# Key-value products of batches 5 to 7 in one quartered stretch with the attention products of batches 4 to 6, in a linear-attention and MLP kernel

## The chip, the cores and the metric

The kernel runs on one core of a Trainium2 chip. The metric is the device time of one launch in microseconds (us); of several executions the median is taken. In the text TensorE does the matmuls, VectorE (DVE in the profile) and ScalarE (ACT) the work on elements, GpSimd (POOL) some more of that, and SyncE (SP) issues most of the DMAs. Each engine takes its instructions in the order in which the program lists them; an instruction that waits holds up all that stand behind it on that engine.

## What is computed

```python
q_s = softmax of q over head_dim          # q, k, v: batch 8, heads 8, seq 576, head_dim 64, float32
k_s = softmax of k over seq
kv  = einsum('bhsd,bhse->bhde', k_s, v)
x   = einsum('bhsd,bhde->bhse', q_s, kv)  # then to (4608 tokens, 512)
h   = x @ w_in                            # 512 x 2048
g   = maximum(0.01 * h, h)
out = g @ w_out                           # 2048 x 512, float32
```

## The kernel before

**The two layers.** The 4608 tokens are taken in nine tiles of 512, t = 0 to 8. In a tile, layer 1 (`layer1`, L488) computes 16 blocks of 128 hidden units, j = 0 to 15: for each j four matmuls of 128x128 weights by 512 columns into one PSUM bank, `ph`, of a pool of six (`psB`). After each j, `leaky` (L497) on ScalarE makes the bf16 activation `gj` from it. Layer 2 (`layer2`, L509) then takes four row groups of 128 tokens, `tsub` = 0 to 3: for each, 16 matmuls, j = 0 to 15, each with `gj` as the weights, into one PSUM bank `pout` of a pool of two. `store` (L503) copies `pout` to `out_sb`, on VectorE nearly always, and SyncE writes it out with two DMAs. Row group 2 reuses the bank of row group 0, and 3 that of 1.

**The attention.** A tile t needs the attention output `xT` of the batches that its tokens lie in. A batch b has 576 tokens, so batch b is attended to in tile b - 1. Its path is this:

- `load_all`: three DMAs on SyncE's queue bring k, q and v of a batch (1152 KB each) into a pool of six raw buffers.
- `k_begin` and `q_begin` take buffers; `k_tree` (L150, four maxima on VectorE), `k_allmax` (L155 to L175, VectorE), `k_sub` (L183, subtract the maximum over the sequence; GpSimd here), `k_exp` (L191, one exponential of 2304 columns on ScalarE).
- `v_cast` (L203, twice 1152 columns, GpSimd): v in bf16, into one of two buffers `vb`.
- `q_max` (L214, VectorE), `q_sub` (L273; GpSimd here), `q_exp` (L281, ScalarE), `q_sum` (L290 and L292), `q_norm` (L297, both VectorE), `q_turn` (L481: a transposing DMA on SyncE's queue gives `qX`).
- `kv` (L310): the key-value product. 72 matmuls, each of 64x64 weights in one quarter of TensorE's array, by 65 columns (the 65th is a column of ones: it gives the softmax sums), into two PSUM banks `pkv`. `kd_make` (L329, L330; VectorE) divides by the sums: four small instructions.
- `attend_all` (L429): the attention product, 8 matmuls of 64x64 weights by 512 columns and 8 by 64, also in quarters, into six PSUM banks `po`. Six `x_keep` casts (L452, ScalarE) bring them to `xT`.

A "quartered stretch" in what follows is a run of such 64x64 matmuls between the 128x128 ones of the two layers.

**What sets the order.** It is written out by hand: `at(t, u, ...)` hangs functions on a place in tile t. u = 0 to 15 is the place right after the activation of j = u in layer 1; u = 16 + 4*tsub + i, i = 0 to 3, is in row group tsub of layer 2, after its matmul 4*i + 3. So u = 19, 23, 27 and 31 are the ends of the row groups, right after that group's `store`; u of 32 and more goes on into the next tile. The functions' instructions enter each engine's queue at that place. `plan(b, o)` hangs batch b's path from place o of tile b - 2 on: o is 27 for batch 3, 22 for batch 4, and 17 for 5 to 7. Batches 0 to 2 are set apart.

Of the kernel before, what the change touches and what calls it, by code (L numbers as in the profile page):

```python
# [8 lines left out]
FP32 = mybir.dt.float32  # L9
# [10 lines left out]
L = 64  # L20
R = 9
# [4 lines left out]
def kernel(  # L26
# [9 lines left out]
    nc = tc.nc  # L36
# [3 lines left out]
    B, H, S, D = q.shape  # L40
# [6 lines left out]
    P = 128  # L47
# [83 lines left out]
    def k_begin(b):  # L131
        st[b]["ke"] = ke_pool.tile([P, R, HL, D], BF16, name="ke")
        st[b]["kmax"] = mx_pool.tile([P, HL, D], FP32, name="kmax")
        st[b]["kmaxT"] = mx_pool.tile([P, HL * D], FP32, name="kmaxT")
        st[b]["kall"] = mx_pool.tile([P, HL, D], FP32, name="kall")

    def k_tree(b, hs, steps=slice(0, 4)):
        n = hs.stop - hs.start
        ks = st[b]["k"][:, hs]
        if steps.start == 0:  # L140
            st[b]["t4"] = mx_pool.tile([P, HL, 4, D], FP32, name="t4")[:, 0:n]
        t4 = st[b]["t4"]
        t2, t1 = t4[:, :, 0:2], t4[:, :, 0]
        for o, i0, i1 in (
            (t4, ks[:, :, 0:4], ks[:, :, 4:8]),
            (t2, t2, t4[:, :, 2:4]),
            (t1, t1, t4[:, :, 1]),
            (st[b]["kmax"][:, hs], t1, ks[:, :, 8]),
        )[steps]:
            nc.vector.tensor_tensor(out=o, in0=i0, in1=i1, op=ALU.max)  # L150

    def k_allmax(b):


        nc.vector.transpose(  # L155
            out=st[b]["kmaxT"], in_=st[b]["kmax"].rearrange("p h d -> p (h d)")
        )
        m2 = small_pool.tile([P, CB, 2], FP32, name="m2")
        nc.vector.tensor_reduce(
            out=m2[:, :, 0],  # L160
            in_=st[b]["kmaxT"].rearrange("p (c j) -> p c j", j=32),
            axis=AX.X,
            op=ALU.max,
        )
        for a in range(4):
            o = a ^ 1
            nc.vector.tensor_reduce(
                out=m2[32 * o : 32 * o + 32, :, 1],
                in_=m2[32 * a : 32 * a + 32, :, 0:1],
                axis=AX.X,  # L170
                op=ALU.max,
            )
        m = small_pool.tile([P, CB], FP32, name="m")
        nc.vector.tensor_reduce(out=m, in_=m2, axis=AX.X, op=ALU.max)
        nc.vector.transpose(  # L175
            out=st[b]["kall"].rearrange("p h d -> p (h d)"),
            in_=m.unsqueeze(2).to_broadcast([P, CB, 32]),
        )

    def k_sub(eng, b, hs):  # L180
        ks = st[b]["k"][:, hs]
        n = hs.stop - hs.start
        eng.tensor_tensor(  # L183
            out=ks,
            in0=ks,
            in1=st[b]["kall"][:, hs].unsqueeze(2).to_broadcast([P, n, R, D]),
            op=ALU.subtract,
        )

    def k_exp(b, hs):  # L190
        nc.scalar.activation(  # L191
            out=st[b]["ke"][:, :, hs].rearrange("p r h d -> p h r d"),
            in_=st[b]["k"][:, hs],
            func=AF.Exp,
        )

    def v_cast(eng, b, gg):
        o = vb2[b % 2][:, :, gg, :, 0:D].rearrange("p r h d -> p h r d")
        i = st[b]["v"][:, 2 * gg : 2 * gg + 2]
        if eng is nc.scalar:  # L200
            eng.copy(out=o, in_=i)
        else:
            eng.tensor_copy(out=o, in_=i)  # L203


    def q_begin(b):
        st[b]["qe"] = qe_pool.tile([P, R, HL, D], BF16, name="qe")
        if b < 2:
            st[b]["qT"] = qT_pool.tile([P, NB, R, L], BF16, name="qT", tag="qT")

    def q_max(b, rs, hs=ALLH):
        n, m = rs.stop - rs.start, hs.stop - hs.start
        st[b]["qmax", rs.start, hs.start] = o = small_pool.tile([P, HL, n], FP32, name="qmax")[:, 0:m]
        nc.vector.tensor_reduce(out=o, in_=st[b]["q"][:, hs, rs], axis=AX.X, op=ALU.max)  # L214
# [55 lines left out]
    def q_sub(eng, b, rs, hs=ALLH):  # L270
        n, m = rs.stop - rs.start, hs.stop - hs.start
        qs = st[b]["q"][:, hs, rs]
        eng.tensor_tensor(  # L273
            out=qs,
            in0=qs,
            in1=st[b]["qmax", rs.start, hs.start].unsqueeze(3).to_broadcast([P, m, n, D]),
            op=ALU.subtract,
        )

    def q_exp(b, rs, hs=ALLH):  # L280
        nc.scalar.activation(  # L281
            out=st[b]["qe"][:, rs, hs].rearrange("p r h d -> p h r d"),
            in_=st[b]["q"][:, hs, rs],
            func=AF.Exp,
        )

    def q_sum(b, rs, hs=ALLH):
        n, m = rs.stop - rs.start, hs.stop - hs.start
        qsum = small_pool.tile([P, n, HL], FP32, name="qsum")[:, :, 0:m]
        nc.vector.reduce_sum(out=qsum, in_=st[b]["qe"][:, rs, hs], axis=AX.X)  # L290
        st[b]["qrec", rs.start, hs.start] = qrec = small_pool.tile([P, n, HL], FP32, name="qrec")[:, :, 0:m]
        nc.vector.reciprocal(out=qrec, in_=qsum)  # L292

    def q_norm(b, rs, hs=ALLH):
        n, m = rs.stop - rs.start, hs.stop - hs.start
        qes = st[b]["qe"][:, rs, hs]
        nc.vector.tensor_tensor(  # L297
            out=qes,
            in0=qes,
            in1=st[b]["qrec", rs.start, hs.start].unsqueeze(3).to_broadcast([P, n, m, D]),  # L300
            op=ALU.mult,
        )
# [15 lines left out]
    def kv(b):  # L318

        pkv = [psB_pool.tile([P, 2, D + 2], FP32, name="pkv", tag=BANK_TAG) for _ in range(2)]  # L320
        for gg in range(2):
            kv_quads(b, gg, [pkv[hh][:, gg] for hh in range(2)])
        st[b]["pkv"] = pkv

    def kd_make(b):
        for hh in range(2):
            pkv = st[b]["pkv"][hh]
            krec = small_pool.tile([P, 2, 1], FP32, name="krec")
            nc.vector.reciprocal(out=krec, in_=pkv[:, :, D : D + 1])  # L329
            nc.vector.tensor_tensor(  # L330
                out=kd2[b % 2][:, :, hh],
                in0=pkv[:, :, 0:D],
                in1=krec.to_broadcast([P, 2, D]),
                op=ALU.mult,
            )
# [110 lines left out]
    def x_keep(eng, b, ggs, rows, hp):  # L446
# [6 lines left out]
        else:  # L453
            eng.tensor_copy(out=o, in_=ps)

    def attend_rows(b, rows, engs=(nc.scalar, nc.scalar)):
        groups = ((0, 1),) if rows.stop - rows.start <= 4 else ((0,), (1,))
        for ggs in groups:
            attend(b, ggs, rows)
        return [  # L460
            lambda ggs=ggs, hp=hp: x_keep(engs[hp], b, ggs, rows, hp) for ggs in groups for hp in range(2)
        ]
# [15 lines left out]
    def q_turn(b, rs=ALLR):  # L478
        if rs.start == 0:
            st[b]["qX"] = qT_pool.tile([P, R * 2, P], BF16, name="qX", tag="qT")  # L480
        nc.sync.dma_start_transpose(  # L481
            out=st[b]["qX"][:, 2 * rs.start : 2 * rs.stop],
            in_=st[b]["qe"][:, rs].rearrange("p r h d -> p (r h d)"),
        )
# [35 lines left out]
    def at(t, u, *fns):  # L520
        while t > 0 and u >= 32:
            t, u = t + 1, u - 32
        hooks.setdefault((t, u), []).extend(fns)
# [7 lines left out]
    def load_all(b):  # L531
        whole = [(ALLH, ALLR)]
        st[b]["k"] = load(k, b, "k_raw", whole)
        st[b]["q"] = load(q, b, "q_raw", whole)
        st[b]["v"] = load(v, b, "v_raw", whole)
# [98 lines left out]

    XR = (slice(0, 6), slice(6, R))
    for b in range(3, B):
        at(b - 2, 2, lambda b=b: load_all(b))

    def plan(b, o):
        t = b - 2  # L640
        at(t, o, lambda: k_begin(b), lambda: q_begin(b), lambda: k_tree(b, ALLH))
        at(t, o + 3, lambda: k_allmax(b), lambda: k_sub(nc.gpsimd, b, ALLH))
        at(t, o + 7, lambda: q_max(b, ALLR), lambda: q_sub(nc.gpsimd, b, ALLR))
        at(t, o + 11, lambda: k_exp(b, ALLH))
        at(t, o + 12, lambda: v_cast(nc.gpsimd, b, 0), lambda: v_cast(nc.gpsimd, b, 1))
        at(t, o + 16, lambda: q_exp(b, ALLR))
        at(t, o + 18, lambda: q_sum(b, ALLR))
        at(t, o + 21, lambda: q_norm(b, ALLR))
        kvu = o + (24 if b == 3 else 25)
        at(t, kvu, lambda: kv(b))  # L650
        at(t, kvu + 1, lambda: kd_make(b))
        at(t, o + 22, lambda: q_turn(b))
        at(b - 1, 27 if b < 5 else 23, lambda: attend_all(b, (slice(0, 8),), (slice(8, R),)))


    def plan2():
        b = 2
# [13 lines left out]
        at(2, 19, lambda: attend_all(b, (XR[1],)))  # L671

    plan2()
    for b in range(3, B):
        plan(b, {3: 27, 4: 22}.get(b, 17))


    def g_tiles():
# [125 lines left out]
```

## Time and profile before

| what | value |
|---|---|
| median of 3 runs | 284.82 us (284.78 to 285.58) |
| the profiled execution, its time | 285.1 us |
| its span, first to last instruction | 283.3 us |
| what lies around the span | 1.8 us |
| TensorE busy | 273.4 us, 96% |
| ScalarE, VectorE, GpSimd busy | 145.5, 142.5, 89.5 us |
| granted TensorE clock over the span | 0.998 |
| chain that ended last: lines L488 and L509 | 38% each |

A line of the timeline gives start, duration, engine, line of the code, operation, result and inputs, shape, and how many were merged; in brackets, how long the engine was idle before, and what released it. Merged pieces overlap a little in time, because instructions are pipelined. The long shares of TensorE's two layers on the chain say that most of the time is one matmul after another; what lies before tile 1 (loads and the first batches) is not touched by the change.

### The profile page before, as it was taken

Reading aid. Unit: us, or ns where it says so; the run is one execution under the profiler, and the core shown is the slowest. Engines: PE = TensorE matmul, PEld = TensorE weight load, DVE = VectorE, ACT = ScalarE, POOL = GpSimd, SP = SyncE. Lnnn points to the kernel's source line nnn. Section 1 sums busy time; section 2 is a strip of 40 time slices with the busy share of each in tenths; the row PEclk is TensorE's granted clock in tenths of the full one; section 3 lists DMA queues with packets and bytes.
Section 4 is the critical chain, followed back from the end, with each engine's and each line's share of the span. In section 5 each row is a group of like instructions: output and inputs, shape, how many; then the busy total and the mean of one; then the engine's idle time right before and its main releaser. Section 6 shows DMA issues by size and latency. Waiting matters only on the chain.

```text
span 283.3 us, 4965 instructions
## 1 busy us (share of the span) xinstructions
PE 273.4 (96%) x1995; PEld 133.3 (47%) x2022; DVE 142.5 (50%) x237; ACT 145.5 (51%) x258; POOL 89.5 (32%) x62
## 2 busy tenths in 40 slices
PE   8889999999999999999999999999999999999994
PEld 3378644444444544444444444444444444444443
DVE  3975984997860992597193718381711100110011
ACT  4976653775359336912973367435843165026400
POOL 2946660035078029308700680059000000000000
PEclk9999999999999999999999999999999999999999
DMA  7999999894969165943598349933052210230033
GB/s 242 335 208 337 285 179 390 264 345 168 174 161 398 31 144 154 405 90 76 119 402 140 74 84 387 188 76 73 1 86 65 61 24 0 65 81 6 0 76 74
DMA packets 37159, 45.81 MB, mean 162 GB/s; under 512 B 16016, under 2 KB 20368, under 8 KB 37136
## 3 DMA queue, kind: packets, MB, share of 16 engines
q1 hardware_dynamic: 33664, 41.16, 49.6%
q0 software_dynamic: 3312, 4.20, 8.4%
q8 instruction: 16, 0.26, 0.4%
q10 hardware_dynamic: 160, 0.13, 0.2%
q14 instruction: 7, 0.06, 0.1%
HBM read 36.70 MB, written 9.44 MB: 163 GB/s over the span
## 4 chain that ended last, share of the span: by engine, by line
PE 80%; DMA 11%; POOL 3%; ACT 2%; DVE 1%; issue 1%; SPq 0%; ACTq 0%; POOLq 0%
PE ph L488 38%; PE pout L509 38%; DMA w_out_sb<-in_moe_w_out_dram 4%; DMA w_in_sb<-in_moe_w_in_dram 3%; DMA k_raw<-in_k_dram 2%; PE po L429 2%; DMA qX<-qe 2%; PE pkv L310 2%; POOL w_in_sb L123 1%; ACT gj L497 1%; DVE qe L297 1%; DVE qsum L290 1%; POOL w_out_sb L128 1%; ACT qe L281 0%; POOL vb L203 0%
## 5 line engine op out<-in xcount | busy, mean ns | idle before, releaser
L488 PE MATMUL ph<-xT,w_in_sb 128*128 128x512 bf16 (+1 forms) x627 | 126.5, 357 | 1.3 <-DMA w_in_sb<-in_moe_w_in_dram 0.6
L509 PE MATMUL pout<-w_out_sb,gj 128*128 128x512 bf16 (+2 forms) x579 | 126.6, 373 | 1.1 <-DMA w_out_sb<-in_moe_w_out_dram 0.6
L497 ACT ACTIVATE gj<-ph 128x512 bf16<-128x512 f32 x144 | 81.3, 604 | 52.4 <-PE ph L488 52.0
L488 PEld LDWEIGHTS <-w_in_sb 128*128 128x128 bf16 x640 | 62.1, 98 | 62.2 <-DMA w_in_sb<-in_moe_w_in_dram 0.8
L509 PEld LDWEIGHTS <-gj 128*128 128x128 bf16 x592 | 56.3, 98 | 65.5 <-issue 1.0
L503 DVE COPY out_sb<-pout 128x512 f32<-128x512 f32 (+1 forms) x34 | 22.7, 675 | 88.6 <-PE pout L509 82.0
L183 POOL TENSOR_TENSOR k_raw<-k_raw,kall 128x2304 f32<-128x2304 f32 (+1 forms) x6 | 29.1, 4854 | 74.9 <-DVE kall L175 60.9
L452 ACT CAST xT<-po 128x512 bf16<-128x512 f32 (+3 forms) x43 | 17.0, 489 | 44.5 <-PE po L429 44.5
L273 POOL TENSOR_TENSOR q_raw<-q_raw,qmax 128x2304 f32<-128x2304 f32 (+4 forms) x12 | 32.3, 2692 | 22.9 <-DVE qmax L214 22.2
L290 DVE TENSOR_REDUCE qsum<-qe 128x36 f32<-128x2304 bf16 (+5 forms) x13 | 20.1, 1544 | 31.4 <-ACT qe L281 31.4
L297 DVE TENSOR_TENSOR qe<-qe,qrec 128x2304 bf16<-128x2304 bf16 (+5 forms) x13 | 22.1, 1698 | 0.4
L191 ACT ACTIVATE ke<-k_raw 128x2304 bf16<-128x2304 f32 (+2 forms) x11 | 17.6, 1602 | 7.8 <-POOL k_raw L183 5.2
L214 DVE TENSOR_REDUCE qmax<-q_raw 128x36 f32<-128x2304 f32 (+5 forms) x13 | 19.9, 1536 | 0.0
L281 ACT ACTIVATE qe<-q_raw 128x2304 bf16<-128x2304 f32 (+5 forms) x13 | 17.3, 1329 | 3.2 <-POOL q_raw L273 3.2
L203 POOL CAST vb<-v_raw 128x1152 bf16<-128x1152 f32 x14 | 15.9, 1166 | 0.0
L150 DVE TENSOR_TENSOR t<-k_raw 128x1024 f32<-128x1024 f32 (+1 forms) x10 | 10.1, 1006 | 2.0 <-DMA k_raw<-in_k_dram 1.8
L150 DVE TENSOR_TENSOR t<-t 128x256 f32<-128x256 f32 (+2 forms) x20 | 9.6, 478 | 0.6
L341 PE MATMUL pout<-zero 128*128 128x512 bf16 x23 | 8.1, 492 | 1.4 <-POOL zero L98 1.3
L503 ACT COPY out_sb<-pout 128x512 f32<-128x512 f32 (+1 forms) x3 | 1.6, 544 | 14.4 <-PE pout L509 14.4
L310 PEld LDWEIGHTS <-ke 64*64 64x64 bf16 x576 | 5.7, 106 | 3.2 <-ACT gj L497 1.7
L310 PE MATMUL pkv<-vb,ke 64*64 64x65 bf16 x576 | 6.8, 194 | 0.2
L228 ACT ACTIVATE qe<-q_raw,nmax 128x64 bf16<-128x64 f32 x16 | 5.3, 334 | 3.3 <-DVE nmax L223 3.3
(59 smaller groups left out, 90.4 us busy)
## 6 DMA issues: line engine op xcount, KB each, us to landing
out_dram<-out_sb SPq DMA_DIRECT2D x70, 128.0 KB, 2.4
v_raw<-in_v_dram SPq DMA_DIRECT2D x7, 1152.0 KB, 10.5
k_raw<-in_k_dram SPq DMA_DIRECT2D x6, 1152.0 KB, 5.9
q_raw<-in_q_dram SPq DMA_DIRECT2D x6, 1152.0 KB, 8.1
k_raw<-in_k_dram SPq DMA_DIRECT2D x4, 576.0 KB, 5.5
w_in_sb<-in_moe_w_in_dram POOLq DMA_DIRECT2D x8, 256.0 KB, 7.7
w_out_sb<-in_moe_w_out_dram POOLq DMA_DIRECT2D x6, 256.0 KB, 10.8
v_raw<-in_v_dram SPq DMA_DIRECT2D x2, 576.0 KB, 7.2
```

Of the source, the lines that this page charges most:

```text
L150: nc.vector.tensor_tensor(out=o, in0=i0, in1=i1, op=ALU.max)
L183: eng.tensor_tensor(out=ks, in0=ks, in1=st[b]["kall"][:, hs].unsqueeze(2).to_broadcast([P, n, R, D]), op=ALU.subtract,)
L191: nc.scalar.activation(out=st[b]["ke"][:, :, hs].rearrange("p r h d -> p h r d"), in_=st[b]["k"][:, hs], func=AF.Exp,)
L214: nc.vector.tensor_reduce(out=o, in_=st[b]["q"][:, hs, rs], axis=AX.X, op=ALU.max)
L273: eng.tensor_tensor(out=qs, in0=qs, in1=st[b]["qmax", rs.start, hs.start].unsqueeze(3).to_broadcast([P, m, n, D]), op=ALU.subtract,)
L290: nc.vector.reduce_sum(out=qsum, in_=st[b]["qe"][:, rs, hs], axis=AX.X)
L297: nc.vector.tensor_tensor(out=qes, in0=qes, in1=st[b]["qrec", rs.start, hs.start].unsqueeze(3).to_broadcast([P, n, m, D]), op=ALU.mult,)
L310: nc.tensor.matmul(outs[hh][hp * D : (hp + 1) * D, 0 : D + 1], lhsT=st[b]["ke"][rows, r, 2 * gg + hp], rhs=vb2[b % 2][rows, r, gg, hp, 0 : ...
L488: nc.tensor.matmul(ph, lhsT=w_in_sb[:, cb, j * P : (j + 1) * P], rhs=xT[:, cb, c0 : c0 + n], start=(cb == 0 and first), stop=(cb == NB - 1 ...
L497: nc.scalar.activation(out=o, in_=ph, func=AF.Prelu, alpha=LEAKY_SLOPE)
L503: copy(out=out_sb, in_=pout)
L509: nc.tensor.matmul(pout, lhsT=g_sb[j // 2][:, j % 2, tsub * P : (tsub + 1) * P], rhs=w_out_sb[:, j, os], start=(j == 0), stop=(j == NF - 1),)
```

## The change

A new `attend_kv(b)` issues, in one place, the 8 attention matmuls of 512 columns of batch b, then the 8 of 64 columns, then all 72 key-value matmuls of batch b + 1, then `kd_make(b + 1)` and the six `x_keep`. The 64-column attention part and the key-value product share two banks, `pokv`, so that six banks are enough. It stands in place of `attend_all` for batches 4, 5 and 6, and of `kv` for 5, 6 and 7. `kv(4)` and attention of batch 7 stay alone.

For that, the k and v path of batches 5 to 7 ends earlier, and the plan is written anew. The subtraction `k_sub` of batches 4 to 7 and `q_sub` of batches 3 to 7 are done by VectorE in place of GpSimd. `load_all` of batches 5 to 7 moves from (b - 2, 2) to (b - 3, 20).

```diff
+    def attend_kv(b, rows=slice(0, 8), rest=slice(8, R)):
+        keep = attend_rows(b, rows)
+        n = 2 * (rest.stop - rest.start) * L
+        both = [psB_pool.tile([P, n + 2 * (D + 2)], FP32, name="pokv", tag=BANK_TAG) for _ in range(2)]
+        ps = [a[:, 0:n].rearrange("p (g c) -> p g c", g=2) for a in both]
+        st[b + 1]["pkv"] = pkv = [a[:, n:].rearrange("p (g d) -> p g d", g=2) for a in both]
+        for gg in range(2):
+            cross(b, gg, [ps[hp][:, gg] for hp in range(2)], rest)
+        for gg in range(2):
+            kv_quads(b + 1, gg, [pkv[hh][:, gg] for hh in range(2)])
+        st[b]["po", (0, 1), rest.start] = ps
+        kd_make(b + 1)
+        for fn in keep:
+            fn()
+        for hp in range(2):
+            x_keep(nc.scalar, b, (0, 1), rest, hp)
...
-        at(b - 2, 2, lambda b=b: load_all(b))
-
-    def plan(b, o):
-        t = b - 2
-        at(t, o, lambda: k_begin(b), lambda: q_begin(b), lambda: k_tree(b, ALLH))
-        at(t, o + 3, lambda: k_allmax(b), lambda: k_sub(nc.gpsimd, b, ALLH))
-        at(t, o + 7, lambda: q_max(b, ALLR), lambda: q_sub(nc.gpsimd, b, ALLR))
-        at(t, o + 11, lambda: k_exp(b, ALLH))
-        at(t, o + 12, lambda: v_cast(nc.gpsimd, b, 0), lambda: v_cast(nc.gpsimd, b, 1))
-        at(t, o + 16, lambda: q_exp(b, ALLR))
-        at(t, o + 18, lambda: q_sum(b, ALLR))
-        at(t, o + 21, lambda: q_norm(b, ALLR))
-        kvu = o + (24 if b == 3 else 25)
-        at(t, kvu, lambda: kv(b))
-        at(t, kvu + 1, lambda: kd_make(b))
-        at(t, o + 22, lambda: q_turn(b))
-        at(b - 1, 27 if b < 5 else 23, lambda: attend_all(b, (slice(0, 8),), (slice(8, R),)))
-
+        at(*((b - 2, 2) if b < 5 else (b - 3, 20)), lambda b=b: load_all(b))
+
+    def plan3():
+        b = 3
+        at(1, 27, lambda: k_begin(b), lambda: q_begin(b), lambda: k_tree(b, ALLH))
+        at(1, 30, lambda: k_allmax(b), lambda: k_sub(nc.gpsimd, b, ALLH))
+        at(2, 2, lambda: q_max(b, ALLR), lambda: q_sub(nc.vector, b, ALLR))
+        at(2, 9, lambda: k_exp(b, ALLH))
+        at(2, 7, lambda: v_cast(nc.gpsimd, b, 0), lambda: v_cast(nc.gpsimd, b, 1))
+        at(2, 11, lambda: q_exp(b, ALLR))
+        at(2, 13, lambda: q_sum(b, ALLR))
+        at(2, 16, lambda: q_norm(b, ALLR))
+        at(2, 17, lambda: q_turn(b))
+        at(2, 19, lambda: kv(b))
+        at(2, 20, lambda: kd_make(b))
+        at(2, 27, lambda: attend_all(b, (slice(0, 8),), (slice(8, R),)))
+
+    def k_front(b, t, u, v):
+        at(t, u, lambda: k_begin(b), lambda: q_begin(b), lambda: k_tree(b, ALLH))
+        at(*v, lambda: k_allmax(b), lambda: k_sub(nc.vector, b, ALLH))
+
+    def q_front(b, t, u):
+        at(t, u, lambda: q_max(b, ALLR), lambda: q_sub(nc.vector, b, ALLR))
+
+    def casts(b, t, u):
+        at(t, u, lambda: v_cast(nc.gpsimd, b, 0), lambda: v_cast(nc.gpsimd, b, 1))
+
+    def q_back(b, t, u):
+        at(t, u, lambda: q_sum(b, ALLR), lambda: q_norm(b, ALLR), lambda: q_turn(b))
+
+    def plan_rest():
+        k_front(4, 2, 9, (2, 21))
+        q_front(4, 2, 29)
+        at(3, 1, lambda: k_exp(4, ALLH))
+        casts(4, 3, 0)
+        at(3, 6, lambda: q_exp(4, ALLR))
+        k_front(5, 3, 5, (3, 14))
+        q_back(4, 3, 9)
+        at(3, 15, lambda: kv(4), lambda: kd_make(4))
+        casts(5, 3, 15)
+        at(3, 22, lambda: k_exp(5, ALLH))
+        at(3, 27, lambda: attend_kv(4))
+        for b in range(5, B):
+            t = b - 1
+            q_front(b, t - 1, 29)
+            at(t, 2, lambda b=b: q_exp(b, ALLR))
+            q_back(b, t, 5)
+            if b + 1 < B:
+                k_front(b + 1, t, 1, (t, 6))
+                casts(b + 1, t, 10)
+                at(t, 14, lambda b=b: k_exp(b + 1, ALLH))
+                at(t, 23, lambda b=b: attend_kv(b))
+            else:
+                at(t, 23, lambda b=b: attend_all(b, (slice(0, 8),), (slice(8, R),)))
```

Where both plans name the same place for the same work, only the engine differs. For batch 3, `k_exp` moves from (2, 6) to (2, 9). For batch 4, tree and subtraction move from (2, 22) and (2, 25) to (2, 9) and (2, 21). For batch 6, to name one of the rest: `k_tree` from (4, 17) to (4, 1), `k_allmax` and `k_sub` from (4, 20) to (4, 6), `k_exp` from (4, 28), in layer 2, to (4, 14), and the key-value product from (5, 10) to (4, 23).

More of the change, by code (lines that the diff above doesn't have):

```diff
@@ L673 @@
     plan2()
-    for b in range(3, B):
-        plan(b, {3: 27, 4: 22}.get(b, 17))
+    plan3()
+    plan_rest()
     def g_tiles():
```

## The prediction

> **What bounds the kernel now.** I read first the busy shares of the page, then TensorE's timeline, to see where it does something other than the two layers, then the timelines of ScalarE and VectorE inside one tile.
>
> ```profile
> PE 273.4 (96%) x1995; PEld 133.3 (47%) x2022; DVE 142.5 (50%) x237; ACT 145.5 (51%) x258; POOL 89.5 (32%) x62
> ```
> ```profile
> 165.89 9.66 PE L488 MATMUL ph<-xT,w_in_sb 128*128 128x512 bf16 x43
> 175.48 0.78 PE L310 MATMUL pkv<-vb,ke 64*64 64x65 bf16 x72
> ...
> 187.52 0.69 PE L429 MATMUL po<-qX,kd 64*64 64x512 bf16 x16
> 188.14 7.08 PE L509 MATMUL pout<-w_out_sb,gj 128*128 128x512 bf16 x32
> 195.05 9.66 PE L488 MATMUL ph<-xT,w_in_sb 128*128 128x512 bf16 x43
> ...
> 224.22 13.98 PE L488 MATMUL ph<-xT,w_in_sb 128*128 128x512 bf16 x62
> ...
> 251.84 13.98 PE L488 MATMUL ph<-xT,w_in_sb 128*128 128x512 bf16 x63
> ```
>
> TensorE is the bound: from tile 2 on, one piece follows the other with no bracket for idle time, except 0.6 us in tile 1. Tiles 2 to 8 begin at 78.10, 107.51, 136.70, 165.89, 195.05, 224.22 and 251.84. Tile 7 has nothing but the two layers, 128 matmuls in 27.62 us, so 0.216 us each, 0.864 us for one j of layer 1 (four), 13.82 us for layer 1, 3.455 us for one row group of layer 2. Tiles 3 to 6 last 29.19, 29.19, 29.16 and 29.17: a key-value product and an attention product, apart, cost 1.55 us together. So a gain must come out of these 1.55 us, and any new wait of TensorE is a loss in full. All that follows counts from the beginning of a tile ("tile 4 + 5.4").
>
> **What the merging saves.** Nothing is taken from TensorE's work: 72 and 16 quartered matmuls stay; three stretches (key-value of 5, 6, 7) go. The trace has one stretch that is shared already, in tile 2: eight attention matmuls of 192 columns, then 72 key-value ones. Tile 2 lasts 29.41, 0.22 longer than tile 3, which lacks only those eight. Alone they would cost two rounds of 192 columns, 2 x 192/512 x 0.216 = 0.16, plus what a stretch costs beyond its columns. That is, for the attention at 132.62: layer 2 from 122.15 to 133.24 is 11.09, less 48 matmuls 10.37, 0.72; its columns, 2 x (512+64)/512 x 0.216 = 0.49; so 0.23. Apart 0.39, in common 0.22: 0.17 saved. Three times, **-0.5 us**. Bounds: 0 (the overhead stays) and 2 x 0.23 = 0.46 a time, -1.4.
>
> **What moves on VectorE.** Subtractions of 2304 columns go from GpSimd (5.07 us for k, 4.05 for q) to VectorE: k of 4 to 7, and, which the few words leave out, q of 3 to 7. No row shows this form. The nearest: k of 1152 columns 1.36, of q 256 columns 0.43, and the same kind of multiplication over 2304, 2.56. I take 2.56 from the last (the first two, extended by 1.04 ns a column, give it too); bounds 2.5 and, twice 1152, 2.7. VectorE is half idle, so these nine cost nothing by themselves; the price is what stands behind them in its queue and ScalarE's, which run in order.
>
> ```profile
> 109.44 0.60 ACT L497 ACTIVATE gj<-ph 128x512 bf16<-128x512 f32 x1 [0.27 <-PE ph L488]
> 109.93 2.12 ACT L191 ACTIVATE ke<-k_raw 128x2304 bf16<-128x2304 f32 x1
> 111.94 2.54 ACT L497 ACTIVATE gj<-ph 128x512 bf16<-128x512 f32 x5
> ```
> ```profile
> 116.52 2.55 DVE L290 TENSOR_REDUCE qsum<-qe 128x36 f32<-128x2304 bf16 x1 [8.12 <-ACT qe L281]
> 119.11 0.38 DVE L292 RECIPROCAL qrec<-qsum 128x36 f32<-128x36 f32 x1
> 119.52 2.56 DVE L297 TENSOR_TENSOR qe<-qe,qrec 128x2304 bf16<-128x2304 bf16 x1
> ```
>
> From the first: the activation of j starts 0.2 after its last matmul (107.51 + 1.73 + 0.2), an exponential holds ScalarE 2.0, and activations that are late follow at 0.48 each. From the second: sum to end of norm, 5.5.
>
> **Tile 4, the exponential before the last activation.** k_exp(6) now stands between the activations of j = 14 and 15, and waits for k_sub(6) on VectorE. The chain: q_exp(5), after j = 2, starts at 3 x 0.864 + 0.2 + 0.5 = 3.3 and ends at 5.4. VectorE comes from q_front(5), which waits behind kd_make(5), that is behind the shared stretch that ends one row group (3.455) before tile 4: krec at -3.4, four small operations 0.8, q_max 2.5, q_sub 2.5 (each next starts 0.1 before the end), so it is free at 2.4; the copy of row group 3, 0.6, to 3.0; k_tree(6), 2.8 (98.37 to 101.15), to 5.7; q_sum to norm 5.5, to 11.2; k_allmax 2.3 (101.75 to 104.01), to 13.5; k_sub 2.56, to 16.0. k_exp 2.0, the last activation 0.6: gj 15 is there at 18.7. TensorE wants it after 15 matmuls of layer 2, at 13.82 + 3.24 = 17.06, and everything behind it there waits: **+1.7 us**. Before, k_exp stood in layer 2 with no activation behind it (192.29, after its wait of 1.93 for GpSimd).
>
> **The casts that meet the tree.** load_all(6) is moved ahead, from the next tile's layer 1 into layer 2 of tile 3, behind the first store in SP's queue: that copy ends at tile 3 + 20.7 (behind k_sub(5) and kd_make(4)), two stores, then k, q, v at 0.55 each, v issued at 23.0, landed 10.3 later (median of the v loads), tile 4 + 3.5. Then GpSimd casts v, twice 1.15, just while k_tree(6) runs (3.0 to 5.7). Rows that tell what such a meeting does:
>
> ```profile
> 62.59 1.72 DVE L297 TENSOR_TENSOR qe<-qe,qrec 128x512 bf16<-128x512 bf16 x1
> ```
> ```profile
> 39.01 1.34 POOL L203 CAST vb<-v_raw 128x1152 bf16<-128x1152 f32 x1
> ...
> 61.00 2.76 POOL L273 TENSOR_TENSOR q_raw<-q_raw,qmax 128x1536 f32<-128x1536 f32 x1 [10.87 <-DVE qmax L214]
> ```
>
> The norm of 512 columns takes 0.69 at 18.22, with GpSimd quiet. At 62.59 GpSimd is in an operation that ends at 63.7, and the norm ends 0.6 after that: it waited for all of it. The reverse at 32.77: a GpSimd subtraction beside one of VectorE takes 3.79, which is its 2.5 (half of 5.07) after the other's end. A cast beside a norm (39.01) took 0.2 longer. Reductions and copies from PSUM show none of it. [...] From the rows I take that they alternate: operation, cast, operation, cast, and the tree ends 2 x 1.15 = **2.3 us** later, all of which reaches gj 15. Bounds: 0 and 2.3.
>
> **Tile 5**, k_exp(7) likewise. q_front(6) stands behind the copy of row group 2, not the stretch: free at 2.3, so gj 15 at 18.6, **+1.6**. Casts of 7: v lands 13.3 after row group 0's end (0.2 + 0.7 + 1.1 + 1.0 + 10.3), and tile 5 begins 3 x 3.455 + 1.4 = 11.75 after it, so at +1.6, while q_sub(6) runs (to 2.3); then cast, tree (0.6 late), cast, tree: **+1.7**. Bounds 0 and 2.3. Tile 6 has no k left, tile 3 has its k_exp(5) in layer 2 (k_sub ends at 19.5, key-value at 25): no wait there; the casts of 5 meet the tree of 5, which has 3 us to spare before q_sum(4).
>
> **Tile 2, a copy behind a subtraction.** k_exp(3) stands after j = 9 instead of 6, so q_exp(3) ends at 92.6 (87.4 + 2.0 + two activations 1.0 + 2.15) instead of 91.46: 1.1 later go q_sum, norm, the copy of row group 0, and kd_make(3), which ended by 98.4; k_allmax(4) at 99.5, k_sub(4) at 101.7, and behind these, newly, the copy of row group 1, 104.2 to 104.9. Row group 3 needs its pout and would start at 104.05: **+0.9**. (Bounds 0.6 and 2.) The last activations, 94.4, are in time for 95.15. q_sub(3) meets GpSimd's k_sub(3) until 84.5 and ends at 87: k_tree(4) and the casts then finish by 92.2, just before q_sum.
>
> At nothing I cost: q_turn, whose transposing DMA is issued at most 1.1 later (attention of 3 at 103.4, landing 3.9 after 98.3; cover gone, it falls into the 0.9 first); stores behind the loads (a buffer is reused a tile later); GpSimd freed of nine subtractions, for which nobody on the path waited.
>
> **Sum**, on the profiled execution (285.1, span 283.3): -0.5 + 0.9 + 1.7 + 2.3 + 1.6 + 1.7 = +7.7, 292.8; that execution is 0.3 above the median 284.82, so **292.5**.
>
> **Rivals.** (1) Casts don't hold up the tree, or v lands too late for it: -0.5 + 0.9 + 1.7 + 1.6 = +3.7, 288.5; one cast a tile instead of two, 290.8. For it: the only cast beside a norm lost 0.2 itself; against it: all two-input pairs in the trace wait. (2) Not slower: VectorE's chain ends early enough. It decides where k_exp(6) starts by 17.06 - 2.6 = 14.4; then only -0.5 and perhaps 0.9 are left, 284.3 to 285.2. The sum after q_exp alone (5.4 + 5.5 + 2.3 + 2.5 = 15.7) speaks against it; it needs rows a fifth shorter than the trace's. (3) The tile-2 wait grows: if a DMA slowed by the loads lands qX(3) late or tree and casts push q_sum(3), up to 1.5 more, 294.
>
> **Chances.** Forecast with alternation (290.8 to 293) 0.54; rival 1 without casts 0.28; rival 2 0.07, of which 0.03 faster by over 0.3%; rival 3 0.11. About 0.3% is what a measurement of this kernel can tell from no change. Range 288 to 294: it takes in rival 1 and leaves out rival 2 and some of what lies above. Faster 0.03, same 0.06, slower 0.91.
>
> **What would show it.** After: TensorE idle in tiles 4 and 5 ahead of layer 2's sixteenth matmul, put to ScalarE's gj; k_exp with a bracket of 2 to 5 us naming VectorE's k_raw; tree operations longer than 1.22 and 0.69 beside casts; a wait for out_sb before row group 3 of tile 2; tiles 2 to 6 at 30.3, 29.8 (27.62 with one key-value product of 0.8 and a shared stretch of 1.4), 33.0, 32.3 and 28.3 (attention alone). The prediction is wrong if tiles 4 and 5 stay under 29.5.

## The result: 295.09 us, slower, by more than forecast

The changed kernel takes 295.09 us (294.38 to 295.70, 4 runs) against 285.12 for the kernel before in the same comparison: 1.0351 times as long, 95% interval 1.0332 to 1.0370. The forecast was 292.5 with a range of 288 to 294. The direction was right and the range was missed by 1.1 us.

The profiled execution took 295.04 us, span 293.3. From its page, busy times and the chain that ended last by engine, and then the view of the core, its span and the mean of the granted TensorE clock:

```profile
PE 277.5 (95%) x2022; PEld 134.0 (46%) x2022; DVE 171.8 (59%) x246; ACT 145.7 (50%) x258; POOL 55.9 (19%) x53
...
PE 59%; DVE 16%; DMA 12%; ACT 4%; issue 4%; POOL 3%; SPq 0%; ACTq 0%; DVEq 0%; POOLq 0%
```
```profile
core 0: 293.3 us, clock 0.988
```

GpSimd's 34 us less and VectorE's 29 us more are for the most part the moved subtractions: they took 40.5 us on GpSimd and take 25.0 on VectorE. Against that, GpSimd's casts now take 6.4 us longer in all and VectorE's tree operations 4.6, of which more below. VectorE now has 16% of the chain, where it had 1%. And the mean clock is 0.988 where it was 0.998: in the page's row of the clock by slices of 7.3 us, two slices (from 154 to 169 us) show 7 tenths, and every slice before the change shows 9 (90% or more). The timeline of TensorE in tiles 4 and 5 shows where (layer 2 is L526 now):

```profile
138.49 13.98 PE L505 MATMUL ph<-xT,w_in_sb 128*128 128x512 bf16 x64
152.30 3.40 PE L526 MATMUL pout<-w_out_sb,gj 128*128 128x512 bf16 x15
159.12 6.66 PE L526 MATMUL pout<-w_out_sb,gj 128*128 128x512 bf16 x17 [3.42 <-ACT gj L514]
165.71 0.63 PE L429 MATMUL po<-qX,kd 64*64 64x512 bf16 x8
...
173.92 13.98 PE L505 MATMUL ph<-xT,w_in_sb 128*128 128x512 bf16 x64
187.73 3.40 PE L526 MATMUL pout<-w_out_sb,gj 128*128 128x512 bf16 x15
193.90 3.84 PE L526 MATMUL pout<-w_out_sb,gj 128*128 128x512 bf16 x17 [2.76 <-ACT gj L514]
```

Twice layer 2 stops after exactly 15 matmuls and waits for gj, as forecast. But the 17 matmuls that follow take 3.84 us in tile 5 and 6.66 in tile 4, for the same work: 2.8 more. Here is the length of each tile, from one beginning of layer 1 to the next, with the experiments below:

| tile | before | after | forecast | vlate | kexp16 | mended | fill_both |
|---|---|---|---|---|---|---|---|
| 2 | 29.41 | 30.66 | 30.3 | 30.67 | 30.95 | 29.41 | 30.75 |
| 3 | 29.19 | 29.89 | 29.8 | 29.89 | 29.89 | 29.88 | 29.89 |
| 4 | 29.19 | 35.43 | 33.0 | 30.98 | 29.02 | 29.03 | 32.62 |
| 5 | 29.16 | 31.93 | 32.3 | 30.75 | 28.99 | 28.99 | 32.54 |
| 6 | 29.17 | 28.35 | 28.3 | 28.35 | 28.35 | 28.35 | 28.35 |

Nearly all of the difference between forecast and result is in tile 4. (In kexp16 tile 2 began 0.3 us earlier than in after, and ended at the same time.) The wait of tile 2 stands in front of its row group 3, as forecast, and names the copy:

```profile
105.15 3.61 PE L526 MATMUL pout<-w_out_sb,gj 128*128 128x512 bf16 x16 [0.76 <-DVE out_sb L520]
```

How the chain of tile 4 ran, first on VectorE and GpSimd, then on ScalarE (bracket: idle before, and who ended it):

```profile
141.01 0.68 DVE L520 COPY out_sb<-pout 128x512 f32<-128x512 f32 x1
141.62 1.21 DVE L150 TENSOR_TENSOR t<-k_raw 128x1024 f32<-128x1024 f32 x1
142.86 1.97 DVE L150 TENSOR_TENSOR t<-t 128x512 f32<-128x512 f32 x2
144.87 1.25 DVE L150 TENSOR_TENSOR kmax<-t,k_raw 128x256 f32<-128x256 f32 x1
146.04 2.54 DVE L290 TENSOR_REDUCE qsum<-qe 128x36 f32<-128x2304 bf16 x1
...
153.87 2.56 DVE L183 TENSOR_TENSOR k_raw<-k_raw,kall 128x2304 f32<-128x2304 f32 x1
```
```profile
143.33 2.52 POOL L203 CAST vb<-v_raw 128x1152 bf16<-128x1152 f32 x2 [26.97 <-DMA v_raw<-in_v_dram]
```
```profile
151.70 0.60 ACT L514 ACTIVATE gj<-ph 128x512 bf16<-128x512 f32 x1 [0.33 <-PE ph L505]
156.46 2.12 ACT L191 ACTIVATE ke<-k_raw 128x2304 bf16<-128x2304 f32 x1 [4.17 <-DVE k_raw L183]
158.49 0.58 ACT L514 ACTIVATE gj<-ph 128x512 bf16<-128x512 f32 x1
```

The tree's second and third operations take 1.97 together and the fourth 1.25 (1.15 and 0.42 in tile 3, with GpSimd quiet), just while the casts run. The subtraction, in the form that no row of before showed, takes 2.56. ScalarE has done j = 14, stands 4.17 us in front of the exponential, and only then makes the last activation, which is there at 159.07.

Last, busy times in stretches around the wait of tile 4 (PE, PEld, DVE, ACT, POOL; then the granted clock, third column from the end, DMA share and GB/s):

```profile
154.00:155.70 1.70, 1.70 (x8) 0.59 (x6) 1.70 (x1) 0.00 (x0) 0.00 (x0) 1.00 0.79 179
155.70:159.10 3.40, 0.00 (x0) 0.00 (x0) 0.73 (x1) 2.61 (x2) 0.00 (x0) 0.84 0.00 0
159.10:160.00 0.90, 0.88 (x3) 0.33 (x4) 0.23 (x1) 0.00 (x0) 0.00 (x0) 0.50 0.00 0
...
164.00:165.00 1.00, 1.00 (x4) 0.33 (x3) 0.00 (x0) 0.00 (x0) 0.00 (x0) 0.57 1.02 369
165.00:166.00 1.00, 1.00 (x12) 0.36 (x14) 0.18 (x1) 0.00 (x0) 0.00 (x0) 1.00 1.02 382
```

The wait itself, in stretches of half a microsecond:

```profile
157.50:158.00 0.50, 0.00 (x0) 0.00 (x0) 0.00 (x0) 0.50 (x1) 0.00 (x0) 1.00 0.00 0
158.00:158.50 0.50, 0.00 (x0) 0.00 (x0) 0.00 (x0) 0.50 (x2) 0.00 (x0) 0.54 0.00 0
```

The clock is halved within the idle time, at 158.04, and comes back some 5.8 us after TensorE's work has. So the theory to be tested had three parts: the activation behind the exponential (tiles 4 and 5), the casts that lengthen it, and a clock that an idle time of this length lets fall. Rivals: the 17 matmuls were slow for another reason; casts and tree don't matter; VectorE's full queue, or the subtractions themselves, are the loss.

### The profile page after: what moved, and what is told of

Its sections match the earlier page's. It is cut to its first block, busy times and chain, and to the rows that moved or that the text cites. A ratio compares the mean times of both kernels' runs of the same rounds, so it can differ in the third digit from the quotient of the medians.

```text
span 293.3 us, 4992 instructions
## 1 busy us (share of the span) xinstructions
PE 277.5 (95%) x2022; PEld 134.0 (46%) x2022; DVE 171.8 (59%) x246; ACT 145.7 (50%) x258; POOL 55.9 (19%) x53
## 4 chain that ended last, share of the span: by engine, by line
PE 59%; DVE 16%; DMA 12%; ACT 4%; issue 4%; POOL 3%; SPq 0%; ACTq 0%; DVEq 0%; POOLq 0%
PE pout L526 30%; PE ph L505 26%; DMA w_out_sb<-in_moe_w_out_dram 4%; DVE qsum L290 3%; DMA w_in_sb<-in_moe_w_in_dram 3%; DVE qe L297 2%; DVE t L150 2%; DMA k_raw<-in_k_dram 2%; DVE k_raw L183 2%; ACT gj L514 2%; DVE qmax L214 2%; ACT ke L191 2%; DMA qX<-qe 1%; POOL w_in_sb L123 1%; DVE out_sb L520 1%
## 5 line engine op out<-in xcount | busy, mean ns | idle before, releaser
L526 PE MATMUL pout<-w_out_sb,gj 128*128 128x512 bf16 (+2 forms) x592 | 131.2, 379 | 7.7 <-ACT gj L514 6.2
L526 PEld LDWEIGHTS <-gj 128*128 128x128 bf16 x592 | 57.0, 99 | 75.2 <-ACT gj L514 7.2
L203 POOL CAST vb<-v_raw 128x1152 bf16<-128x1152 f32 x14 | 22.4, 1620 | 77.4 <-DMA v_raw<-in_v_dram 77.4
L452 ACT CAST xT<-po 128x512 bf16<-128x512 f32 (+3 forms) x37 | 16.0, 517 | 34.5 <-PE po L429 34.5
L273 POOL TENSOR_TENSOR q_raw<-q_raw,qmax 128x512 f32<-128x512 f32 (+3 forms) x7 | 12.0, 1721 | 23.0 <-DVE qmax L214 22.3
L273 DVE TENSOR_TENSOR q_raw<-q_raw,qmax 128x2304 f32<-128x2304 f32 (+1 forms) x6 | 15.2, 2536 | 0.2
L183 DVE TENSOR_TENSOR k_raw<-k_raw,kall 128x2304 f32<-128x2304 f32 (+1 forms) x7 | 14.2, 2043 | 0.3
L150 DVE TENSOR_TENSOR t<-k_raw 128x1024 f32<-128x1024 f32 (+1 forms) x10 | 11.3, 1135 | 2.2 <-DMA k_raw<-in_k_dram 2.0
L150 DVE TENSOR_TENSOR t<-t 128x256 f32<-128x256 f32 (+2 forms) x20 | 12.0, 601 | 0.6
L183 POOL TENSOR_TENSOR k_raw<-k_raw,kall 128x1152 f32<-128x1152 f32 (+1 forms) x2 | 8.9, 4433 | 12.1 <-DMA out_dram<-out_sb 11.6
```

Source lines behind the costliest of these rows:

```text
L183: eng.tensor_tensor(out=ks, in0=ks, in1=st[b]["kall"][:, hs].unsqueeze(2).to_broadcast([P, n, R, D]), op=ALU.subtract,)
L273: eng.tensor_tensor(out=qs, in0=qs, in1=st[b]["qmax", rs.start, hs.start].unsqueeze(3).to_broadcast([P, m, n, D]), op=ALU.subtract,)
L526: nc.tensor.matmul(pout, lhsT=g_sb[j // 2][:, j % 2, tsub * P : (tsub + 1) * P], rhs=w_out_sb[:, j, os], start=(j == 0), stop=(j == NF - 1),)
```

## The experiments

**kexp16: the exponential behind the last activation.**

```diff
-                at(t, 14, lambda b=b: k_exp(b + 1, ALLH))
+                at(t, 16, lambda b=b: k_exp(b + 1, ALLH))
```

> The changed kernel with k_exp of batches 6 and 7 at place 16 (in row group 0) instead of 14, so behind the activation of j = 15 on ScalarE. Theory (the whole loss of tiles 4 and 5 is that one activation behind k_exp, with the clock): both tiles last 29.0, 295.1 - 3.4 - 3.0 - 2.9 = 285.8, and the 1.2 of tile 2 stay. Rival (VectorE's queue is too long in itself: the key-value product or the copies of row groups 0 and 1 wait for it next): part of the wait comes back at the shared stretch, 287 to 290.

Measured: 285.84 us, ratio 1.0039 (1.0027 to 1.0051); tiles 4 and 5 at 29.02 and 28.99, no bracket on TensorE in either, clock 1.00. One place in ScalarE's order, in two tiles, is 9.3 us. The rival falls: the exponential still waits 2.54 us for VectorE, but nothing that TensorE wants soon is behind it.

**vlate: v of batches 6 and 7 loaded later.**

```diff
...
-        at(*((b - 2, 2) if b < 5 else (b - 3, 20)), lambda b=b: load_all(b))
+        at(*((b - 2, 2) if b < 5 else (b - 3, 20)), lambda b=b: load_all(b, b > 5))
+        if b > 5:
+            at(b - 2, 0, lambda b=b: load_v(b))
```

The second argument makes `load_all` leave v out; `load_v` loads it.

> The changed kernel with the v loads of batches 6 and 7 issued at place 0 of tile 4 (5) instead of with k and q in row group 1 of the tile before, so that GpSimd's casts no longer fall into the tree of VectorE. Theory (cast and two-input operation exclude each other; the tree of tile 4 took 4.4 us instead of 2.8, that of tile 5 3.95): the tree takes 2.8 in both, TensorE's wait in tile 4 falls from 3.4 to 1.8 and in tile 5 from 2.8 to 1.6, and with 1.8 us of idle time the clock stays: 295.1 - 1.6 - 1.2 - 3.1 = 289.2. Rival (casts and tree don't hurt each other): the waits stay, 295.1. Rival (the clock falls all the same): 292.2.

Measured: 289.61 us, ratio 1.0169 (1.0149 to 1.0189), clock 1.00. The tree is back at its length, the waits for gj are 1.78 and 1.59:

```profile
157.47 3.84 PE L526 MATMUL pout<-w_out_sb,gj 128*128 128x512 bf16 x17 [1.78 <-ACT gj L514]
...
188.26 3.84 PE L526 MATMUL pout<-w_out_sb,gj 128*128 128x512 bf16 x17 [1.59 <-ACT gj L514]
```

VectorE in tile 4 of this kernel, then GpSimd:

```profile
141.61 1.22 DVE L150 TENSOR_TENSOR t<-k_raw 128x1024 f32<-128x1024 f32 x1
142.86 1.15 DVE L150 TENSOR_TENSOR t<-t 128x512 f32<-128x512 f32 x2
144.04 0.43 DVE L150 TENSOR_TENSOR kmax<-t,k_raw 128x256 f32<-128x256 f32 x1
...
147.38 2.56 DVE L297 TENSOR_TENSOR qe<-qe,qrec 128x2304 bf16<-128x2304 bf16 x1
```
```profile
148.65 3.39 POOL L203 CAST vb<-v_raw 128x1152 bf16<-128x1152 f32 x2 [31.34 <-DMA v_raw<-in_v_dram]
```

The casts meet the norm instead, which began first: it keeps its 2.56, and they take 3.39 in place of 2.24. In these rows whoever is second waits. So the casts' share of the waits is 3.42 - 1.78 = 1.6 us in tile 4 and 2.76 - 1.59 = 1.2 in tile 5. With the clock's 2.8, which the longer wait of tile 4 brought with it, that is the difference up to 295.1.

**fill14, fill2, fill_both: zeros in the wait.** Matmuls of zeros, whose result nobody reads, stand between j = 14 and j = 15 of row group 0; nothing else is changed. The edit is that of fill14; fill2 has 2 in place of 14, fill_both has 12 and `t in (4, 5)`.

```diff
                 layer2(po, g_sb, tsub, j)
+                if t == 4 and tsub == 0 and j == NF - 2:
+                    fill = psB_pool.tile([P, TT], FP32, name="fill", tag=BANK_TAG)
+                    for i in range(14):
+                        nc.tensor.matmul(fill, lhsT=zero[:, 0:P], rhs=zero, start=(i == 0), stop=(i == 13))
```

> The changed kernel with 14 matmuls of zeros (128x512, into a PSUM bank of their own, read by nobody) on TensorE in row group 0 of tile 4, between the matmuls of j = 14 and j = 15, so that the wait of 3.42 us for the last activation is filled with 3.0 us of work. Theory (TensorE's granted clock falls to a half after the idle time of 3.42 us, and the 17 matmuls behind it take 6.66 us in place of 3.7 for that reason alone): the clock stays at 1.00, tile 4 lasts 32.4 instead of 35.4, the time is 292.1. Rival (the 17 matmuls are slow by what they read or by other traffic, or wait by themselves): 295.1 as before. Rival (the idle time does no harm and the zeros only cost): above 295.

> The same with two matmuls of zeros, 0.43 us, so that the idle time is 3.0 us, between the 2.76 of tile 5, after which the clock stayed, and the 3.42 of tile 4, after which it fell. If only the length of the idle time counts and 3.0 is short enough: 292.1 in every execution and clock 1.00. If it depends also on where the idle time falls: executions of both kinds, 292 and 295. If 3.0 is long enough: 295.1.

Measured: fill14 294.55 us, ratio 1.0343 (1.0325 to 1.0361); fill2 294.63 (three executions near 294.5 with clocks of 0.991 to 0.994, one at 296.44 with 0.986), 1.0363 (1.0325 to 1.0401). As times, both expectations of 292.1 failed. The timeline of fill14, tiles 4 and 5, tells why:

```profile
155.81 3.19 PE L825 MATMUL fill<-zero 128*128 128x512 bf16 x14
159.40 3.84 PE L526 MATMUL pout<-w_out_sb,gj 128*128 128x512 bf16 x17 [0.41 <-ACT gj L514]
...
191.82 5.53 PE L526 MATMUL pout<-w_out_sb,gj 128*128 128x512 bf16 x17 [3.24 <-ACT gj L514]
```

In tile 4 the theory held: the 17 matmuls take 3.84. But now tile 5 waits longer (3.24, not 2.76), and the clock falls there, at 192.8, a microsecond after work has begun again. The reason for the longer wait: with tile 4's end no longer slowed, v of batch 7, loaded from row group 1 of tile 4 on, lands later within tile 5 and its casts hit more of the tree, the second and third operation 2.80 together. In fill2 an idle time of 3.00 in tile 4 went without a fall, and again tile 5 had 3.24 and fell. A run that fills both waits was needed. (The lengths so far, 2.76 and 3.00 without a fall and 3.24 and 3.42 with one, could still go by a threshold; the moment of the fall speaks against it: 2.34 us into the wait in the changed kernel, after work had begun again here. More in the last section.)

> The changed kernel with 12 matmuls of zeros in the wait of tile 4 and 12 in that of tile 5. With the wait of tile 4 alone filled, the clock stayed there and fell in tile 5 instead, whose wait had grown from 2.76 to 3.24 us; the time hardly moved. Theory (idle time of 3.2 us and more lets the clock fall, and nothing else makes matmuls slow): clock 1.00 throughout, 17 matmuls behind each wait in 3.84 us, tile 4 at 32.4 and tile 5 at 32.3 to 32.7 with the waits for gj as long as before, 285.1 - 0.4 + 1.2 + 3.4 + 3.2 = 292.3 (292 to 292.7). Rival (the loss is not the clock's): 294.5 as before.

Measured: 292.74 us, just above what was expected, ratio 1.0261 (1.0235 to 1.0287), clock 0.999 to 1.000 in all four executions (0.986 to 0.992 in the changed kernel). 17 matmuls take 3.84 behind both waits:

```profile
159.26 3.84 PE L526 MATMUL pout<-w_out_sb,gj 128*128 128x512 bf16 x17 [0.84 <-ACT gj L514]
...
191.83 3.84 PE L526 MATMUL pout<-w_out_sb,gj 128*128 128x512 bf16 x17 [0.79 <-ACT gj L514]
```

So without a fall the kernel takes 292.7. The 2.35 us up to 295.09 are the clock's 2.8, less the 0.6 by which tile 5 is longer here, as it waits longer, like in fill14.

**mended, mended_apart: no wait, and the merging alone.** mended has kexp16's edit and two more for tile 2: `k_exp` of batch 3 goes back to its old place, and `k_allmax` and `k_sub` of batch 4 go behind the copy of row group 1. In mended_apart the key-value products of 5 to 7 then get a stretch of their own. The edit for tile 2:

```diff
-        k_front(4, 2, 9, (2, 21))
+        k_front(4, 2, 9, (2, 24))
...
-        at(2, 9, lambda: k_exp(b, ALLH))
+        at(2, 6, lambda: k_exp(b, ALLH))
```

> k_exp of 6 and 7 behind the last activation (place 16), k_allmax and k_sub of batch 4 at (2, 24), behind the copy of row group 1, and k_exp of batch 3 back at (2, 6). Theory (the three waits are all that the change loses): every tile 2 to 6 without a wait of TensorE, and the shared stretches save 0.13 to 0.17 each: 0.4 to 0.5 under the kernel before, 284.7 if that is 285.1. Rival (the shared stretch saves nothing): 285.1. Rival (a wait that those covered comes up): above 285.5.

> The mended kernel with the key-value products of 5, 6 and 7 in a stretch of their own, one row group after the attention product (at (3, 31), (4, 27), (5, 27)), all else the same. Theory (a stretch of quartered matmuls costs about 0.23 us beside its columns, most of which a shared one saves): 0.4 to 0.5 us more than the mended kernel, as much as the kernel before. Rival (what the mended kernel saves comes from the new order or the subtractions on VectorE): the same as the mended kernel.

Measured, side by side with the kernel before at 285.07 (29 runs): mended 284.73, ratio 0.9987 (0.9978 to 0.9997, 12 runs); mended_apart 285.12, 1.000 (0.999 to 1.001, 12 runs). No bracket on TensorE is left in tiles 2 to 6. From the beginning of tile 2 to that of tile 7 the profiles have 145.66 and 146.18 us: 0.52 for three stretches, 0.17 each. That is what the merging is worth, and mended is the fastest of all, by 0.1%, with an interval that only just leaves out 1. The two edits of tile 2 were made together, so which of them takes the wait away isn't told apart.

**subs_only: the kernel before with the subtractions on VectorE.**

```diff
-        at(t, o + 3, lambda: k_allmax(b), lambda: k_sub(nc.gpsimd, b, ALLH))
-        at(t, o + 7, lambda: q_max(b, ALLR), lambda: q_sub(nc.gpsimd, b, ALLR))
+        at(t, o + 3, lambda: k_allmax(b), lambda: k_sub(nc.vector if b > 3 else nc.gpsimd, b, ALLH))
+        at(t, o + 7, lambda: q_max(b, ALLR), lambda: q_sub(nc.vector, b, ALLR))
```

> The kernel before with one part of the change alone: k_sub of batches 4 to 7 and q_sub of 3 to 7 on VectorE, with the old places, old loads and apart stretches. Theory (VectorE has room; the subtractions cost only by what stands behind them): 285.1, the same, since in the old order the copy of row group 1 ends at 161.2 in tile 4 where it is wanted at 162.7 or later. Rival (the subtractions on VectorE are a loss by themselves): 0.5 to 3 us more.

Measured: 285.12 us, 1.000 (0.999 to 1.001). Moving nine subtractions to VectorE, in the old order, costs nothing and gains nothing by itself.

## Why the prediction was right in kind and too small

- **The merging (-0.5):** right; 0.52 in the profiles of mended and mended_apart, 0.39 between their medians.
- **The exponential before the last activation (+1.7 and +1.6):** right. vlate, where the casts don't interfere, has 1.78 and 1.59; kexp16 has none. TensorE loses another 0.18 each time in starting again (vlate's tile 4 is 1.96 longer than kexp16's), which had no term.
- **The casts in the tree (+2.3 and +1.7):** right in kind; 1.6 and 1.2. They do alternate, operation, cast, operation, cast (in tile 4 one ends after the other, at 143.55, 144.56, 144.84, 145.84 and 146.12), but the price of a cast was too high. Its full 1.15 was the author's estimate from a subtraction ahead of a norm; no row of before has a cast ahead of a VectorE operation, and no run shows that price: the casts came at 143.33, while the second operation ran, and held up the third and fourth by 0.8 each (1.97 - 1.15 and 1.25 - 0.42), not by 1.15; in tile 5 the first lost 0.35 and the next two 0.82 together. Why 0.8 and not a cast's full length, no run shows. That both casts met the tree at all is in part luck: v landed 1.3 us later in tile 4 and 1.1 us earlier in tile 5 than worked out (4.8 and 0.5 into the tile in place of 3.5 and 1.6). In after and vlate a cast and an operation of VectorE held each other up in both directions: 1.25 against 0.42 for the tree's last operation beside a cast, 3.39 against 2.24 for two casts behind the norm.
- **The copy behind the subtraction in tile 2 (+0.9):** 1.25. It was there, and its wait too, "0.76 <-DVE out_sb". The rest of 0.35 is mostly that v of batch 4, whose landing the working had not placed, came at 93.6, and its casts held up the norm of batch 3 (2.85 in place of 2.56). Rival 3's late qX came as well, 0.36 us, but lies in front of the same wait and adds nothing to its end.
- **What had no term at all: the clock.** The sum let TensorE go on after a wait at 0.216 us a matmul. After 3.42 us idle it went on at half the clock: 17 matmuls in 6.66 instead of 3.84 us, +2.8. That is the step that failed, in the sum itself. fill_both shows it: without a fall 292.74. That this is so near the forecast's 292.5 is in part luck, since the price of the casts, too high, makes up for the 0.4 of starting again and the 0.4 that tile 2 took beyond its term there. The page of before, with TensorE's clock at 9 in every slice, hides such a fall, but its trace has one, behind the last matmul, which ends at 279.67; in the line below a mean of 0.62 over half a microsecond puts the fall at 282.12, after 2.45 us without work. The working never asked what a wait of 4 us does to the engine that waits.

```profile
282.00:282.50 0.50, 0.00 (x0) 0.00 (x0) 0.00 (x0) 0.00 (x0) 0.00 (x0) 0.62 0.00 0
```

- **Rivals:** 1 (casts don't matter, 288.5) is near what vlate makes on purpose, 289.6, and fell for the change itself. 2 (not slower) fell: k_sub ended at tile 4 + 17.9. 3 fell as a price: tile 2 took 0.35 more than forecast, not up to 1.5.

The tiles of after add up: from the beginning of tile 2 to that of tile 7, 156.26 us against 146.12, +10.1; the forecast's +7.7, plus 2.8 for the clock, 0.4 for starting again, 0.3 for tile 2, less 1.1 for shorter waits in tiles 4 and 5 (3.42 and 2.76 in place of 4.0 and 3.3).

## What to carry to other kernels

Before an instruction is hung between two others of an in-order engine, write down when its input is ready and what stands behind it: here an exponential a place too early, in two tiles, made two late activations and 9.3 us. The gain of moving work into a shared stretch (0.17 us each, 0.5 in all) was right and small; the order that came with it cost some twenty times as much, 10.5 us. When a forecast has the bound engine wait for microseconds, price also how it comes back: the wait of 3.42 us cost 6.4.

## What the runs showed of the hardware

**The clock was halved for 3.41 us or twice that, and the length of an idle time alone did not tell when.** The granted clock was 0.50 from 158.04 to 164.87 in the changed kernel, from 192.83 to 196.24 in fill14 and from 191.93 to 195.33 in fill2 (worked out from the granted clock in stretches of 0.2 to 1 us): 6.83, 3.41 and 3.40, so two, one and one times 3.41. The length of an idle time doesn't order the cases: the clock fell 2.34 us into the wait of tile 4 in the changed kernel, but 3.00 us in fill2 went without a fall, and so did the last 3.6 us of mended (its last matmul ends at 279.39, and the clock is at 1.00 up to the span's end at 283.0):

```profile
282.00:283.00 1.00, 0.00 (x0) 0.00 (x0) 0.00 (x0) 0.00 (x0) 0.00 (x0) 1.00 0.00 0
```

Counted in steps of 3.41 us from the ends of the half clock, the step before each fall had 2.3, 2.4 and 2.9 us idle. The idle times without a fall lie across a border of two steps: 3.00 in fill2 as 1.8 and 1.2, 2.76 in tile 5 of after as 1.0 and 1.7. And the clock came back after the first step without idle time. The ends of fill14 and fill2 agree with it: behind the last matmul the clock falls again at 291.82 and 290.91 (the mean over the span is 0.992 and 0.991), in both 95.6 us after it had come back, which is 28 steps. In fill2 the step before that fall had 2.05 us idle and 1.36 us of work, the least idle time that was followed by a fall here; the 1.8 us in its tile 4 were not. That the clock is decided in such steps is an estimate from these few falls, and no run tried it by shifting an idle time on purpose.

**Matmuls of zeros kept the clock up**: with 12 of them in each wait (fill_both) it was 0.999 to 1.000 over the span, and the waits left were 0.84 and 0.79 us. They were worth some 2.4 us (292.74 against 295.09, each beside a kernel before at 285.29 and 285.12); without the waits there is nothing to fill.
